# Weight sums kept in DRAM as float32 and split on the way back, with re-laid DRAM rows, new planner constants and a wider warm-up

## The chip, the cores and the metric

The kernel runs on one core of a Trainium2 chip. The time is device microseconds of one execution, from the chip. A profiled execution gives a span (first to last instruction) and the work of each engine: PE (TensorE, matrix products), PEld (its weight loads), DVE (VectorE), ACT (ScalarE), POOL (GpSimd) and SP (SyncE, which here issues nearly all DMAs).

## The reference, cut to what matters

Everything is float32. Attention with random features comes first, then two feed-forward layers:

```
x = phi(q) @ (phi(k)^T v) / (phi(q) @ sum(phi(k)) + 1e-6)   # 4 batches, 8 heads, 576 tokens, head 64, 128 features
phi(x) = exp(x w - |x|^2/2 - max) / sqrt(128)
h = x @ w_in ; g = softplus(h) ; y = g @ w_out              # 2304 tokens, 512 -> 2048 -> 512
h = y @ w_in2 ; g = h * sigmoid(h) ; out = g @ w_out2       # the same sizes
```

## The kernel before, in words

A float32 product is made from three fp32r products. Each operand is held as a high part (the value rounded to fp32r by an ACT copy) and a low part (value minus high part, by a DVE subtraction, `diff`, line 285); the products high·high, high·low and low·high are added up in PSUM.

The matrix work has four stages, one after the other on PE. Stage 1 is `first_layer` (lines 849 to 851): x @ w_in, directly. Between its blocks stand the matmuls of attention (lines 291, 579, 583, 714, 745, 761, 779). Stage 2 is `second_product(0)` (line 977), stage 3 `first_product` (line 1225), stage 4 `second_product(1)` (line 983). Stages 2 to 4 use a 2x2 block scheme with seven products in place of eight (order 1, 5, 6, 2, 7, 3, 4). For it each pair of weight blocks is turned into seven sums, cells of 128x256. There are 24 pairs: eight for each of the three weight matrices, `(0,1)`, `(1,0)` and `(1,1)`.

`sums_of(m, k)` makes the seven cells of a pair. Two raw loads of 512 KB (line 359) hold the weights in a 64-bit form, out of which `unpack` makes float32 (one ACT operation, three DVE operations: lines 364, 368, 373, 378). Four DVE operations add and subtract (line 479). In `stage`, ACT (lines 454, 456) makes the high part of a sum and DVE (lines 285, 461) the low part, three times for two cells together and once for one cell that is negated, and SP stores both parts into the DRAM tensor `ws` (line 466): 256 KB for a cell, 168 cells. For the first 12 pairs the parts are collected in two larger tiles (tag `wb`, constant `APART`), for the others they go out in four stores.

The products load their weights back from `ws`, both parts, in 42 loads of 1 MB (lines 1104 and 1123: 14 for each of the stages 2, 3 and 4). `second_product` takes the weights in two halves `q`; a half is seven tiles, used by three units of tokens (`sc`), and its tiles come free one by one in the last of the three.

In stages 2 and 4 a unit loads four blocks of `gate` (line 899, 768 KB each), DVE combines them (line 910, 1536 columns), ACT and DVE split 14 half-products (lines 925 and 285, 768 columns each) into tiles of tag `wa`, of which there are seven. DVE and ACT take the results out of PSUM (lines 1018, 1024, 1037). In stage 3 the results are gated (lines 1235, 1240, 1245, 1251) and stored in `gate[1]` (line 1258, 192 KB each).

The order of the work on every engine is planned on the host. Each operation is put into an `Order` with its cost in microseconds, the operations it waits for, the buffers it takes and a due time; `Order.run` then plays all engines forward in time and always takes the operation that can start first (nearly equal starts: the earlier due time). A DMA costs its bytes at 360 GB/s plus 2.3 us. Due times come from constants: `BEGIN`, `EVERY` and `SHARE` for attention and stage 1, `PREP` for the 24 pairs, `EARLIER` for how long ahead weights are loaded. What the planner puts out is the program order; on the chip each engine keeps to it and waits on semaphores.

At the start (lines 321 to 325) PE runs two products of 384 columns on zeros ("warm-up", four matmul records) while the first inputs are loaded; the first projection (line 579) waits for `om_sb`.

Of the kernel before, what the change touches and what calls it, by code (L numbers as in the profile page):

```python
# [8 lines left out]
F32 = mybir.dt.float32  # L9
# [35 lines left out]
ROW = {1: 0, 2: 1, 6: 2, 3: 3, 7: 4, 5: 5, 4: 6}  # L45
# [4 lines left out]
STAY = 6.79  # L50
# [6 lines left out]
FROM = {"PE": 4.6, "ACT": 3.4, "DVE": 2.0, "SP": 0.8}  # L57
SLACK = 0.15
EARLY = 6
# [6 lines left out]
BACKLOG, SOON = 0.6, 13.16  # L66
EARLIER = (26.31, 42.98)
APART = 12
AHEAD, WAIT = 3.04, 4.21
RATE = 360e3  # L70
ARRIVE = 2.3
ISSUE = 0.5
BEGIN = 38.66
SHARE = (1.76, 1.19, 1.06, 0.07, 0.19)
PREP = (118.5, 128.9, 155.1, 144.2, 172.5, 186.4, 193.1, 218.5, 239.1, 242.1, 258.9, 272.1, 289.7, 296.7, 311.4, 322.8, 520.9, 537.5, 578.5, 584.0, 604.5, 622.5, 614.1, 638.6)
# [10 lines left out]
def on_dve(n):  # L86
    return (0.067 + n / 960, 0.15)
# [3 lines left out]
class Order:  # L91
# [5 lines left out]
    def add(self, eng, cost, fn, deps=(), due=None, alloc=(), uses=(), table=None, nbytes=0, after=0.0, loose=False, behind=None, wait=0.0, tiled=False, turn=None):  # L97
# [34 lines left out]
    def run(self):  # L132
# [70 lines left out]
        while len(order) < len(items):  # L203
# [63 lines left out]
def attention_moe_moe_kernel(  # L267
# [45 lines left out]
    ws = {m: dram.tile([NFP, 7, P, 2 * 256], F32, name=f"ws{m[0]}{m[1]}") for m in ((0, 1), (1, 0), (1, 1))}  # L313
# [33 lines left out]
    def unpack(layer, fc, io, raw_tag, into, tf, first, after, due=None):  # L347
# [5 lines left out]
        def views():  # L353
            u = s["raw"].bitcast(U32).rearrange("p (n t) -> p n t", t=2)
            return u[:, :, 0], u[:, :, 1]
# [5 lines left out]
        def scale():  # L361
            first()
            hif = s["raw"].bitcast(F32).rearrange("p (n t) -> p n t", t=2)[:, :, 1]
# [17 lines left out]
        a = add("SP", (ISSUE, 0), load, alloc=[traw], nbytes=P * DM * 8, after=after, due=due)  # L381
# [3 lines left out]
        return add("DVE", V5, sign, [d], uses=[traw, tf]), b  # L385

    def weights(fc, after):
# [20 lines left out]
        r, _ = unpack(0, fc, 0, "b4" if e else "rw", lambda: s["f"], tf, begin, after)  # L408
# [5 lines left out]
    def sums_of(m, k, due, apart):  # L414
# [6 lines left out]
        def begin():  # L421
            s["f"] = get("f", [P, 2, DM], F32, f"pair_{name}")

        def row(i):
            return s["f"][:, :, i * 256 : (i + 1) * 256] if io else s["f"][:, i, :].rearrange("p (j w) -> p j w", j=2)

        done, opened = [], None
        for e in range(2):
            r, b = unpack(layer, 2 * k + e, io, "rw", lambda e=e: s["f"][:, e, :], tf, begin if e == 0 else lambda: None, due - 45, due - 16 + 2 * e)
# [4 lines left out]
        kept[m, k] = []  # L434

        group = {}

        def stage(i, of, n, deps, neg, due):
            g = 4 * (i >= 4) if apart else i
            rows = (4, 3)[g // 4] if apart else n  # L440
            tag = "wb" if apart else "rw"
            opens = g not in group
            if opens:
                group[g] = dict(t=new(tag), ends=[], left=rows)
            q = group[g]
            ts = q["t"]
            w = 256 * n

            def high():
                if opens:  # L450
                    q["st"] = get(tag, [P, rows, 2, 256], F32R, f"st_{name}_{g}")
                st = q["st"][:, i - g : i - g + n]
                if neg:
                    nc.scalar.activation(st[:, 0, 0], of()[:, 0], AF.Copy, scale=-1.0)
                else:
                    nc.scalar.copy(st[:, :, 0], of())  # L456

            def low():
                st = q["st"][:, i - g : i - g + n]
                if neg:  # L460
                    nc.vector.scalar_tensor_tensor(st[:, 0, 1], of()[:, 0], -1.0, st[:, 0, 0].bitcast(F32), op0=ALU.mult, op1=ALU.subtract)
                else:
                    diff(st[:, :, 1], of(), st[:, :, 0].bitcast(F32))

            def store():
                nc.sync.dma_start(ws[m][k, g : g + rows].rearrange("o p w -> p o w"), q["st"].bitcast(F32).rearrange("p o h w -> p o (h w)"))

            a = add("ACT", on_act(w), high, deps + ([] if opens else [q["first"]]), alloc=[ts] if opens else [], uses=[tf] + ([] if opens else [ts]))
            if opens:
                q["first"] = a  # L470
            b = add("DVE", on_dve(w), low, [a], uses=[ts, tf])
            q["ends"].append(b)
            q["left"] -= n
            if not q["left"]:
                kept[m, k].append(add("SP", (ISSUE, 0), store, q["ends"], uses=[ts], nbytes=P * 256 * rows * 8, due=due))
            return b

        def one(out, a, b, op, deps):
            return add("DVE", on_dve(256), lambda: nc.vector.tensor_tensor(out(), a(), b(), op=op), deps, uses=[tf])

        def cell(i, j):
            return lambda: row(i)[:, j]

        u = stage(0, lambda: row(0), 2, done, False, due - 5)
        v = stage(6, lambda: row(1)[:, 1:2], 1, done, True, due - 4)
        s1 = one(cell(1, 1), cell(1, 0), cell(1, 1), ALU.add, [v])
        s3 = one(cell(1, 0), cell(0, 0), cell(1, 0), ALU.subtract, [s1])
        stage(4, lambda: row(1), 2, [s3], False, due - 2)
        s2 = one(cell(0, 0), cell(1, 1), cell(0, 0), ALU.subtract, [s3, u])
        s4 = one(cell(0, 1), cell(0, 1), cell(0, 0), ALU.subtract, [s2])  # L490
        stage(2, lambda: row(0), 2, [s4], False, due)
# [7 lines left out]
    def inputs(s, name, xT, xN, vs, fold, held, after):  # L499
# [31 lines left out]
        for i, (v, shape) in enumerate(vs or ()):  # L531
# [12 lines left out]

            lv.append(add("SP", (ISSUE, 0), load_v, rv if tw is here else [] if opens else lv[:1], alloc=[tv[i]] if opens else [], uses=[] if opens else [tv[i]], nbytes=P * VW * 4, after=after))

# [275 lines left out]
    def first_layer(sb):  # L822
# [4 lines left out]
        for fc in range(NFC):  # L827
# [44 lines left out]
            stored[0].setdefault(fc, []).append((cols[sb], cols[sb] + w, add("SP", (ISSUE, 0), store, [a1], due=due + c1 + 4, uses=[tg], nbytes=P * w * 4)))  # L872
# [4 lines left out]
    def second_product(layer, t0):  # L877
# [6 lines left out]
        def unit(q, sc, t0, tws, wload, wt):  # L884
# [6 lines left out]
            def load_b(i, j):  # L891
# [60 lines left out]
            t4 = combine("t", "t", b21, [got[1, 0]] + e2, [tt, tb[1, 0]])  # L952
# [9 lines left out]
            def product(p, r, c, due, deps):  # L962
# [5 lines left out]
                def run(s=s, wt=wt):  # L968
# [4 lines left out]
                    for k in range(2):  # L973
                        if layer == 0:
                            cs = slice(c * P, (c + 1) * P)
                            for a, h in ((0, 0), (0, 1), (1, 0)):
                                nc.tensor.matmul(o[:, :HW_], w[:, 2 * r + k, a, cs], g[:, k, h], start=one, stop=(k == 1 and a == 1), skip_group_check=True)  # L977
                                one = False
                        else:
                            for a in range(2 if c == 0 else 1):  # L980
                                ts = slice((2 * c + a) * P, (2 * c + a + 1) * P)
                                for h, v in ((0, 0), (0, 1), (1, 0)):
                                    nc.tensor.matmul(o[:, a * 256 : a * 256 + 256], g[:, k, h, ts], w[:, 2 * r + k, v], start=one, stop=(k == 1 and h == 1), skip_group_check=True)  # L983
# [19 lines left out]
            def fetch(c, i, j):  # L1003
# [7 lines left out]
                return add("SP", (ISSUE, 0), load, [partly[sc, c, i, j]], alloc=[ht], nbytes=P * wide[c] * 4)  # L1011
# [17 lines left out]
            def finish(p, x, c, i, j, dep, due):  # L1029
# [9 lines left out]
                if not final:  # L1039
                    partly[sc, c, i, j] = add("SP", (ISSUE, 0), lambda s=s: nc.sync.dma_start(part_of(c, i, j), s["h", c, i, j][:, :w]), [e], uses=[ht], due=due + 3, nbytes=P * w * 4)  # L1040
                elif layer == 0:
                    yready[sc, i, j, c] = add("SP", (ISSUE, 0), lambda s=s: nc.sync.dma_start(y_dram[sc, i, j, c], s["h", c, i, j][:, :w]), [e], uses=[ht], due=due + 3, nbytes=P * w * 4)
                else:
                    for a in range(2 - c):
# [7 lines left out]
                        for p0, n, r0 in rows:  # L1052
# [4 lines left out]
                            add("SP", (ISSUE, 0), store, [e], uses=[ht], due=due + 3, nbytes=n * 1024)  # L1057
# [38 lines left out]
        for q in range(NQ):  # L1096
            tws, wload, wt = {}, {}, {}
            for n, p in enumerate(chain):
# [3 lines left out]
                def load_w(p=p, q=q, wt=wt, tag=tag):  # L1102
                    w = wt[p] = get(tag, [P, KQ, 2, 256], F32R, f"w2_{layer}_{q}_{p}")
# [296 lines left out]
```

## Time and profile before

| | before |
|---|---|
| median of 3 runs | 868.63 us (866.46 to 871.35) |
| profiled execution: time / span | 866.67 us / 864.9 us |
| PE busy | 851.5 us, 98% of the span |
| DVE / ACT busy | 681.6 us (79%) / 542.5 us (63%) |
| DMA queue of SP | 253.36 MB, 85% of 16 engines |
| mean granted clock | 1.000 |

"Busy" is the time in which an engine executed something; ends of matmuls are modelled, so neighbouring records overlap. Times in the rows below are microseconds unless marked ns.

### The profile page before, as it was taken

The numbers are of one execution on the slowest core, as the hardware profiler recorded it, in microseconds if no ns is written. First come the engines' busy times: TensorE is split into PE (matmuls) and PEld (weight loads), VectorE is DVE, ScalarE is ACT, GpSimd is POOL, SyncE is SP. The second block draws the span as 40 slices with busy tenths as digits, with TensorE's granted clock in tenths as the row PEclk, the third lists the DMA queues.
The fourth block names the chain that finished last, engine by engine and source line by source line (L and its number), as shares of the span: only waits on it lengthen the run. The fifth ranks groups of instructions, "written<-read, shape, count | busy, mean of one in ns | idle before, by whom it ended". The sixth has DMA issues, their size and how long they took to land.

```text
span 864.9 us, 17428 instructions
## 1 busy us (share of the span) xinstructions
PE 851.5 (98%) x6492; PEld 801.8 (93%) x6492; DVE 681.6 (79%) x1264; ACT 542.5 (63%) x1088; POOL 1.2 (0%) x8
## 2 busy tenths in 40 slices
PE   8899999999999999999999999999999999999998
PEld 7688888888888899999999998999999999999998
DVE  4999989969997377999799943786754899768973
ACT  6977778768765566876575444766855646543430
POOL 0000000000000000000000000000000000000000
PEclk9999999999999999999999999999999999999999
DMA  9576899899989999979995899987699997799532
GB/s 319 203 240 181 259 314 333 305 348 331 311 297 362 344 345 397 366 258 308 358 324 195 279 354 390 328 291 258 224 317 345 383 352 247 252 348 348 167 117 74
DMA packets 150293, 254.54 MB, mean 294 GB/s; under 512 B 10816, under 2 KB 82624, under 8 KB 150208
## 3 DMA queue, kind: packets, MB, share of 16 engines
q1 hardware_dynamic: 150048, 253.36, 85.0%
q8 instruction: 51, 0.84, 0.4%
q14 instruction: 34, 0.28, 0.1%
q10 hardware_dynamic: 160, 0.07, 0.0%
HBM read 152.72 MB, written 100.66 MB: 293 GB/s over the span
## 4 chain that ended last, share of the span: by engine, by line
PE 89%; DMA 5%; DVE 4%; ACT 1%; issue 1%; SPq 0%; ACTq 0%; DVEq 0%
PE X L977 12%; PE X L983 12%; PE X L1225 8%; PE h L849 8%; PE h L851 8%; PE h L850 8%; PE Z L983 6%; PE Z L977 6%; PE Z L1225 4%; PE Y L983 3%; PE Y L977 3%; PE Y L1225 2%; PE pp_q L579 2%; PE pp_k L579 2%; PE pkv_k L291 2%; PE pn_q L291 2%
## 5 line engine op out<-in xcount | busy, mean ns | idle before, releaser
L849 PE MATMUL h<-x,wt 128*128 128x512 f32 (+1 forms) x328 | 123.4, 376 | 0.0
L851 PE MATMUL h<-x,wt 128*128 128x512 f32 (+1 forms) x328 | 119.6, 365 | 0.0
L850 PE MATMUL h<-x,wt 128*128 128x512 f32 (+1 forms) x328 | 119.4, 364 | 0.0
L1225 PE MATMUL X<-x_x,w 128*128 128x384 f32 x576 | 106.6, 335 | 2.7 <-ACT s L1235 2.4
L925 ACT CAST g<-b 128x768 fp32r<-128x768 f32 x96 | 78.3, 838 | 48.4 <-PE X L983 19.2
L983 PE MATMUL X<-w,g 128*128 128x256 f32 x864 | 107.0, 283 | 0.2 <-issue 0.2
L983 PEld LDWEIGHTS X<-w,g 128*128 128x128 f32 x864 | 105.1, 192 | 0.5 <-issue 0.3
L1225 PEld LDWEIGHTS X<-x_x,w 128*128 128x128 f32 x576 | 100.2, 188 | 3.7 <-ACT s L1235 3.1
L977 PE MATMUL X<-g,w 128*128 128x384 f32 x576 | 102.9, 334 | 0.0
L977 PEld LDWEIGHTS X<-g,w 128*128 128x128 f32 x576 | 100.1, 188 | 0.0
L925 ACT CAST g<-t 128x768 fp32r<-128x768 f32 x72 | 58.8, 834 | 65.3 <-DVE t L910 38.1
L285 DVE TENSOR_TENSOR g<-b,g 128x768 fp32r<-128x768 f32 x96 | 90.0, 951 | 11.1 <-ACT g L925 11.1
L285 DVE TENSOR_TENSOR g<-t,g 128x768 fp32r<-128x768 f32 x72 | 67.5, 953 | 21.0 <-ACT g L925 20.7
L849 PEld LDWEIGHTS h<-x,wt 128*128 128x128 f32 x328 | 61.9, 189 | 10.4
L851 PEld LDWEIGHTS h<-x,wt 128*128 128x128 f32 x328 | 61.9, 189 | 10.2
L285 DVE TENSOR_TENSOR st<-pair,st 128x512 fp32r<-128x512 f32 x72 | 48.9, 686 | 27.9 <-ACT st L456 27.8
L850 PEld LDWEIGHTS h<-x,wt 128*128 128x128 f32 x328 | 62.0, 189 | 8.6
L855 ACT COPY g<-h 128x512 f32<-128x512 f32 (+1 forms) x80 | 44.1, 559 | 28.7 <-PE h L851 20.2
L456 ACT CAST st<-pair 128x512 fp32r<-128x512 f32 x72 | 44.8, 629 | 19.3 <-DMA ws<-st 7.7
L983 PE MATMUL Z<-w,g 128*128 128x256 f32 x432 | 54.0, 283 | 0.2 <-DVE g L285 0.2
L1225 PE MATMUL Z<-x_x,w 128*128 128x384 f32 x288 | 53.8, 334 | 0.0
L983 PEld LDWEIGHTS Z<-w,g 128*128 128x128 f32 x432 | 52.8, 192 | 0.4 <-DVE g L285 0.4
(113 smaller groups left out, 1457.0 us busy)
## 6 DMA issues: line engine op xcount, KB each, us to landing
w<-ws SPq DMA_DIRECT2D x42, 1024.0 KB, 7.7
b<-gate SPq DMA_DIRECT2D x48, 768.0 KB, 7.5
raw<-in_w SPq DMA_DIRECT2D x64, 512.0 KB, 6.0
ws<-st SPq DMA_DIRECT2D x36, 512.0 KB, 5.1
gate<-s SPq DMA_DIRECT2D x96, 192.0 KB, 4.6
gate<-g SPq DMA_DIRECT2D x64, 256.0 KB, 5.0
ws<-st SPq DMA_DIRECT2D x12, 1024.0 KB, 7.0
ws<-st SPq DMA_DIRECT2D x12, 768.0 KB, 5.5
```

The lines of the kernel that those rows point to most:

```text
L285: nc.vector.tensor_tensor(o, a, b, op=ALU.subtract)
L291: nc.tensor.matmul(o[r], a[:, r], b, **flags)
L456: nc.scalar.copy(st[:, :, 0], of())
L579: nc.tensor.matmul(pp[j][:, q], s["xt"][r, c : c + P], om_sb[r, :], start=True, stop=not fold)
L849: nc.tensor.matmul(ph, wt[:, 0, cs], xt[:, 0, ts], start=(opens and cc == 0), stop=False, skip_group_check=part is not None)
L850: nc.tensor.matmul(ph, wt[:, 0, cs], xt[:, 1, ts], start=False, stop=False, skip_group_check=part is not None)
L851: nc.tensor.matmul(ph, wt[:, 1, cs], xt[:, 0, ts], start=False, stop=(cc == NCC - 1), skip_group_check=part is not None)
L855: nc.scalar.copy(s["g"][:, :w], s["h"][:, :w])
L925: nc.scalar.copy(g[:, :, 0], s[src][:, 2 * r : 2 * r + 2])
L977: nc.tensor.matmul(o[:, :HW_], w[:, 2 * r + k, a, cs], g[:, k, h], start=one, stop=(k == 1 and a == 1), skip_group_check=True)
L983: nc.tensor.matmul(o[:, a * 256 : a * 256 + 256], g[:, k, h, ts], w[:, 2 * r + k, v], start=one, stop=(k == 1 and h == 1), skip_group_chec ...
L1225: nc.tensor.matmul(s[x][:, :HW_], w[:, a, cs], xop[p][:, cc, h], start=(opens and cc == 0 and a == 0 and h == 0), stop=(cc == 1 and a == 1 ...
```

## The change

Five things change, none of them the number or the shape of the matmuls of stages 1 to 4.

1. `sums_of` no longer splits. It makes the seven cells in float32 (cells 0 to 3 in the tile `f`, 4 to 6 in the second raw tile, whose content is used up by then) with the same four DVE operations, and stores them in two DMAs (512 KB and 384 KB). `APART` and `stage` go. The sign of one cell is turned, and with it one subtraction on the side of the data.
2. Behind each of the 42 loads, now 512 KB, stand a new ACT copy and a new DVE subtraction over 1024 columns (`halve`), before the products may use the tile.
3. `ws` and `gate[1]` are laid out so that a load reads 4 KB (`ws`) or 6 KB (`gate[1]`) in a row for each partition, in place of 2 KB and 1.5 KB. Stores into `ws` write rows of 1 KB for `(0,1)` and `(1,1)`, of 4 and 3 KB for `(1,0)`.
4. The planner costs a DMA by bytes and by rows, and adds 0.97 us behind each DMA that starts after 40.33 us. Its constants are new.
5. The warm-up has 512 columns in place of 384.

```diff
-ROW = {1: 0, 2: 1, 6: 2, 3: 3, 7: 4, 5: 5, 4: 6}
+ROW = {1: 0, 2: 1, 7: 2, 4: 3, 5: 4, 6: 5, 3: 6}
-FROM = {"PE": 4.6, "ACT": 3.4, "DVE": 2.0, "SP": 0.8}
+FROM = {"PE": 5.2, "ACT": 3.6, "DVE": 2.0, "SP": 0.8}
-FIRST = {"k": "by", "q": "yy", "kv": "b", "flip": "b", "num": "b", "back": "y"}
+FIRST = {"k": "by", "q": "yy", "kv": "b", "flip": "b", "num": "y", "back": "y"}
-LEAD, TRAIL, EVERY, WINDOW_OF, FETCH = 0.05, 2.2, 3.13, 25.82, 24.95
+LEAD, TRAIL, EVERY, WINDOW_OF, FETCH = 0.05, 2.36, 2.85, 35.33, 27.18
-EARLIER = (26.31, 42.98)
-APART = 12
+EARLIER = (35.65, 27.02)
+PER_BYTE, PER_ROW = 2.44e-6, 6.35e-4
+MARGIN, FIRM = 0.97, 40.33
-BEGIN = 38.66
-SHARE = (1.76, 1.19, 1.06, 0.07, 0.19)
-PREP = (118.5, 128.9, ... 638.6)
+BEGIN = 29.9
+SHARE = (1.76, 1.19, 1.06, 0.18, 0.41)
+PREP = (105.6, 119.7, ... 635.2)
...
+        nbytes *= RATE * (PER_BYTE + PER_ROW / row)
-                it["end"] = wire + ARRIVE
+                it["end"] = wire + ARRIVE + (MARGIN if s > FIRM else 0.0)
...
-    gate = [dram.tile([NQ, KQ, 2, P, B * S], F32, name=f"gate{i}") for i in range(2)]
+    gate = [dram.tile([NQ, KQ, 2, P, B * S], F32, name="gate0"), dram.tile([NQ, 2, SC, 2, P, KQ, HW_], F32, name="gate1")]
-    ws = {m: dram.tile([NFP, 7, P, 2 * 256], F32, ...
+    ws = {m: dram.tile([P, NFP * 7, 256] if m == (1, 0) else [NQ, 7, P, KQ, 256], F32, ...
-    wz = get("b2", [P, 3 * P], F32, "wz")
+    wz = get("b2", [P, 2 * T], F32, "wz")
-    pw = get("bank", [P, 3 * P], F32, "pw")
+    pw = get("bank", [P, 2 * T], F32, "pw")
...
+        def keep(o, n, of, deps, t, due):
+            return add("SP", (ISSUE, 0), lambda: store(o, n, of), deps, uses=[t], nbytes=P * n * 1024, row=n * 1024 if m == (1, 0) else 1024, due=due)
+        s1 = one(4, 2, 3, ALU.add, done)
+        s3 = one(2, 0, 2, ALU.subtract, [s1])
+        s2 = one(5, 4, 0, ALU.subtract, [s1])
+        s4 = one(6, 1, 5, ALU.subtract, [s2])
+        kept[m, k] = [keep(0, 4, ..., [s3], tf, due - 1), keep(4, 3, ..., [s4], traw, due)]
+
+    def halve(w, tw, dep, cells, due=None):
+        def high():
+            nc.scalar.copy(w()[:, 0], w()[:, 1].bitcast(F32))
+        def low():
+            t = w()
+            diff(t[:, 1], t[:, 1].bitcast(F32), t[:, 0].bitcast(F32))
+        a = add("ACT", on_act(cells * 256), high, [dep], uses=[tw])
+        return add("DVE", on_dve(cells * 256), low, [a], uses=[tw], due=due)
...
-                    w = wt[p] = get(tag, [P, KQ, 2, 256], F32R, ...)
-                    nc.sync.dma_start(w.bitcast(F32)..., ws[wm][q * KQ : (q + 1) * KQ, ROW[p]]...)
+                    w = wt[p] = get(tag, [P, 2, KQ, 256], F32R, ...)
+                    nc.sync.dma_start(w[:, 1].bitcast(F32), ws[wm][q, ROW[p]])
+                wload[p] = halve(lambda p=p, wt=wt: wt[p], tws[p], wl, KQ)
```

## Rows read from the trace of the kernel before

**Rows 1.** The page: busy time of PE, and the DMA queue of SP.

```profile
PE 851.5 (98%) x6492; PEld 801.8 (93%) x6492; DVE 681.6 (79%) x1264; ACT 542.5 (63%) x1088; POOL 1.2 (0%) x8
q1 hardware_dynamic: 150048, 253.36, 85.0%
```

**Rows 2.** Waits of PE: what it waited for, us in total, times, longest.

```profile
PE px_q L779 <- DVE xn_q L771: 3.8, 3, 1.8
PE X L1225 <- ACT s L1235: 2.4, 2, 1.9
PE pw L325 <- POOL ident masks.py:199: 1.8, 1, 1.8
```

**Rows 3.** Busy time by stretch: start:end, length, PE, PEld, DVE, ACT, POOL, clock, DMA share, GB/s.

```profile
20.00:46.00 26.00, 21.26 (x337) 18.04 (x336) 24.97 (x84) 24.41 (x72) 0.00 (x0) 1.00 0.63 222
46.00:326.00 280.00, 280.00 (x2405) 237.77 (x2404) 235.27 (x568) 200.08 (x475) 0.00 (x0) 1.00 0.89 306
413.30:500.70 87.40, 87.40 (x506) 87.40 (x505) 79.52 (x113) 47.40 (x61) 0.00 (x0) 1.00 0.87 290
500.70:545.00 44.30, 42.38 (x245) 42.06 (x244) 15.83 (x30) 21.54 (x45) 0.00 (x0) 1.00 1.03 372
```

**Rows 4.** PE in order of time at the start: start, us, line.

```profile
1.81 2.93 PE L325 MATMUL pw<-wz,ident 128*128 128x384 f32 x4 [1.81 <-POOL ident masks.py:199]
5.21 0.80 PE L579 MATMUL pp_k<-om_sb,x_k 64*128 64x128 f32 x4 [0.47 <-ACT om_sb L320]
...
7.17 0.64 PE L579 MATMUL pp_k<-om_sb,x_k 64*128 64x128 f32 x4
7.60 0.64 PE L583 MATMUL pp_k<-neg_half,x_k 64*128 64x128 f32 x4
...
10.92 0.39 PE L583 MATMUL pp_k<-neg_half,x_k 64*128 64x128 f32 x4
11.14 0.39 PE L579 MATMUL pp_k<-om_sb,x_k 64*128 64x128 f32 x4
```

**Rows 5.** ACT in order of time: the first two exponentials of attention.

```profile
9.85 2.17 ACT L623 ACTIVATE phi_k<-pp_k,mn_k 128x128 f32<-128x128 f32 x8 [1.42 <-DVE mn_k L596]
12.51 2.17 ACT L623 ACTIVATE phi_k<-pp_k,mn_k 128x128 f32<-128x128 f32 x8 [0.49 <-DVE mn_k L596]
```

**Rows 6.** The chain that ended last, around 503 to 540 us.

```profile
502.95 11.38 DMA raw<-in_w
...
519.91 8.74 DMA ws<-st
...
530.80 8.68 DMA gate<-s
```

**Rows 7.** Groups of DVE and ACT: busy us, mean ns, idle before.

```profile
L285 DVE TENSOR_TENSOR g<-b,g 128x768 fp32r<-128x768 f32 x96 | 90.0, 951 | 11.1 <-ACT g L925 11.1
L285 DVE TENSOR_TENSOR st<-pair,st 128x512 fp32r<-128x512 f32 x72 | 48.9, 686 | 27.9 <-ACT st L456 27.8
L910 DVE TENSOR_TENSOR t<-b,b 128x1536 f32<-128x1536 f32 x12 | 21.0, 1752 | 1.0 <-DMA b<-gate 1.0
L1037 DVE TENSOR_TENSOR h<-X,h 128x384 f32<-128x384 f32 (+2 forms) x36 | 19.6, 552 | 13.1 <-PE X L983 8.8 <-PE X L977 4.3
L461 DVE SCALAR_TENSOR_TENSOR st<-pair,st 128x256 fp32r<-128x256 f32 x24 | 10.1, 419 | 4.2 <-ACT st L454 4.0
L925 ACT CAST g<-b 128x768 fp32r<-128x768 f32 x96 | 78.3, 838 | 48.4 <-PE X L983 19.2 <-PE Z L983 9.0 <-PE Y L983 5.2
L456 ACT CAST st<-pair 128x512 fp32r<-128x512 f32 x72 | 44.8, 629 | 19.3 <-DMA ws<-st 7.7 <-DVE pair L479 5.8 <-DMA b<-gate 4.2
L454 ACT ACTIVATE st<-pair 128x256 fp32r<-128x256 f32 x24 | 10.2, 425 | 7.3 <-DVE pair L378 4.3 <-DMA ws<-st 2.7
```

**Rows 8.** DMA issues: count, KB each, median us from issue to landing.

```profile
w<-ws SPq DMA_DIRECT2D x42, 1024.0 KB, 7.7
raw<-in_w SPq DMA_DIRECT2D x64, 512.0 KB, 6.0
```

More of the change, by code (lines that the diff above doesn't have):

```diff
@@ L95, in __init__, with add @@
         self.items = []
-    def add(self, eng, cost, fn, deps=(), due=None, alloc=(), uses=(), table=None, nbytes=0, after=0.0, loose=False, behind=None, wait=0.0, tiled=False, turn=None):
+    def add(self, eng, cost, fn, deps=(), due=None, alloc=(), uses=(), table=None, nbytes=0, after=0.0, loose=False, behind=None, wait=0.0, tiled=False, turn=None, row=2048):
         occ, lag = cost if isinstance(cost, tuple) else (cost, PIPE)
         i = len(self.items)
+        nbytes *= RATE * (PER_BYTE + PER_ROW / row)
         it = dict(
@@ L345, in attention_moe_moe_kernel, with unpack @@
     wready = {}
-    def unpack(layer, fc, io, raw_tag, into, tf, first, after, due=None):
+    def unpack(layer, fc, io, raw_tag, into, tf, first, after, due=None, rows=1):
         s = {}
@@ L380, in unpack @@
         opens = not tf["users"]
-        a = add("SP", (ISSUE, 0), load, alloc=[traw], nbytes=P * DM * 8, after=after, due=due)
+        a = add("SP", (ISSUE, 0), load, alloc=[traw], nbytes=P * DM * 8, row=4096, after=after, due=due)
         b = add("ACT", (0.575, 0.37), scale, [a], alloc=[tf] if opens else [], uses=[traw] + ([] if opens else [tf]))
@@ L384, in unpack @@
         d = add("DVE", V5, low_bits, [b, c], uses=[traw, tf])
-        return add("DVE", V5, sign, [d], uses=[traw, tf]), b
+        return add("DVE", V5, sign, [d], uses=[traw, tf]), b, (s, traw)
     def weights(fc, after):
@@ L433, in sums_of @@
             done.append(r)
[L434 to L488, printed above, removed]
@@ L489, in sums_of, with cell, one @@
-        s2 = one(cell(0, 0), cell(1, 1), cell(0, 0), ALU.subtract, [s3, u])
-        s4 = one(cell(0, 1), cell(0, 1), cell(0, 0), ALU.subtract, [s2])
-        stage(2, lambda: row(0), 2, [s4], False, due)
+        def cell(o):
+            return s["f"][:, o] if o < 4 else sr["raw"].bitcast(F32)[:, (o - 4) * 256 : (o - 3) * 256]
+        def one(o, a, b, op, deps):
+            return add("DVE", on_dve(256), lambda: nc.vector.tensor_tensor(cell(o), cell(a), cell(b), op=op), deps, uses=[tf, traw])
@@ new lines, in sums_of @@
+        s4 = one(6, 1, 5, ALU.subtract, [s2])
+        kept[m, k] = [
+            keep(0, 4, lambda: s["f"], [s3], tf, due - 1),
+            keep(4, 3, lambda: sr["raw"].bitcast(F32)[:, :768].rearrange("p (o w) -> p o w", o=3), [s4], traw, due),
+        ]
+    def halve(w, tw, dep, cells, due=None):
[6 more added lines that the diff above has]
+        return add("DVE", on_dve(cells * 256), low, [a], uses=[tw], due=due)
@@ L543, in load_v @@
                 nc.sync.dma_start(s["v", i], v)
-            lv.append(add("SP", (ISSUE, 0), load_v, rv if tw is here else [] if opens else lv[:1], alloc=[tv[i]] if opens else [], uses=[] if opens else [tv[i]], nbytes=P * VW * 4, after=after))
+            lv.append(add("SP", (ISSUE, 0), load_v, rv if tw is here else [] if opens else lv[:1], alloc=[tv[i]] if opens else [], uses=[] if opens else [tv[i]], nbytes=P * VW * 4, row=1040 if shape[1] == 4 else 2080, after=after))
         def square():
@@ L871, in first_layer @@
             a1 = add("ACT", on_act(w, True), evacuate, [g1], due=due + c1 + 1.6, alloc=[tg], uses=[th])
-            stored[0].setdefault(fc, []).append((cols[sb], cols[sb] + w, add("SP", (ISSUE, 0), store, [a1], due=due + c1 + 4, uses=[tg], nbytes=P * w * 4)))
+            stored[0].setdefault(fc, []).append((cols[sb], cols[sb] + w, add("SP", (ISSUE, 0), store, [a1], due=due + c1 + 4, uses=[tg], nbytes=P * w * 4, row=w * 4)))
     last = [None]
@@ L976, in run @@
                             for a, h in ((0, 0), (0, 1), (1, 0)):
-                                nc.tensor.matmul(o[:, :HW_], w[:, 2 * r + k, a, cs], g[:, k, h], start=one, stop=(k == 1 and a == 1), skip_group_check=True)
+                                nc.tensor.matmul(o[:, :HW_], w[:, a, 2 * r + k, cs], g[:, k, h], start=one, stop=(k == 1 and a == 1), skip_group_check=True)
                                 one = False
@@ L982, in run @@
                                 for h, v in ((0, 0), (0, 1), (1, 0)):
-                                    nc.tensor.matmul(o[:, a * 256 : a * 256 + 256], g[:, k, h, ts], w[:, 2 * r + k, v], start=one, stop=(k == 1 and h == 1), skip_group_check=True)
+                                    nc.tensor.matmul(o[:, a * 256 : a * 256 + 256], g[:, k, h, ts], w[:, v, 2 * r + k], start=one, stop=(k == 1 and h == 1), skip_group_check=True)
                                     one = False
@@ L1055, in store @@
                                 nc.sync.dma_start(out[r0 : r0 + n, cs], s["h", c, i, j][p0 : p0 + n, a * 256 : a * 256 + 256])
-                            add("SP", (ISSUE, 0), store, [e], uses=[ht], due=due + 3, nbytes=n * 1024)
+                            add("SP", (ISSUE, 0), store, [e], uses=[ht], due=due + 3, nbytes=n * 1024, row=1024)
                 return e
@@ L1257, in store @@
                     def store():
-                        nc.sync.dma_start(gate[1][fc // (2 * KQ), fc // 2 % KQ, fc % 2][:, lo : lo + HW_], s[key])
-                    stored[1].setdefault(fc, []).append((lo, lo + HW_, add("SP", (ISSUE, 0), store, [a], uses=[th], due=due + 2.5, nbytes=P * HW_ * 4)))
+                        nc.sync.dma_start(gate[1][fc // (2 * KQ), fc % 2, sc, j, :, fc // 2 % KQ], s[key])
+                    stored[1].setdefault(fc, []).append((lo, lo + HW_, add("SP", (ISSUE, 0), store, [a], uses=[th], due=due + 2.5, nbytes=P * HW_ * 4, row=HW_ * 4)))
                 def step(p, end):
```

67 lines of the change are left out of this document (35 added, 32 removed).

## The prediction, as it was put on record

> **What bounds the kernel now.** I read the page first: PE is busy for 851.5 of 864.9 us, while SP's queue fills 85% of the DMA engines' time [rows 1]. So the first question is what PE loses, not what the DMAs carry: the change touches no matmul behind the start, and all it can win is PE's idle time, 864.9 - 851.5 = 13.4 us, and the time at the start in which PE works at half speed. The waits of PE say whose idle time it is: 3.8 us for attention's normalised values, 2.4 us in stage 3 for ACT, 1.8 us before the warm-up [rows 2]. The stretches say where: from 46 to 326 us PE is busy for all 280 us, from 413.3 to 500.7 us for all 87.4; the idle time stands in 20 to 46 us (26.0 - 21.3 = 4.7) and 500.7 to 545 us (44.3 - 42.4 = 1.9) [rows 3]. In the first of these DVE is busy for 25.0 of 26.0 us, in the second DVE for only 15.8 and the DMA engines all the time, at 372 GB/s [rows 3]. The granted clock reads 1.00 in these rows, so the slow start has to be read from the pitch: a group of four projection matmuls starts each 0.43 us (7.17 to 7.60) and later each 0.22 us (10.92 to 11.14) [rows 4]. [...]
>
> **The change, part by part.** I sum against the profiled execution, 866.67 us, which lies 1.96 us under the median of the runs shown, 868.63.
>
> *Splits.* Removed are 72 ACT and 72 DVE operations over 512 columns and 24 each over 256: on ACT 44.8 + 10.2 = 55.0 us, on DVE 48.9 + 10.1 = 59.0 [rows 7]. Added are 42 of each over 1024 columns, a size that no row shows. From below it is bounded by the 768-column rows, 838 ns on ACT and 951 on DVE, from above by the 1536-column DVE row, 1752 [rows 7]. Along the line between the DVE rows 1024 columns cost 951 + 256 * (1752 - 951) / 768 = 1218 ns; on ACT the step from 512 to 768 columns, 838 - 629 = 209, gives 1047. So ACT gains 55.0 - 42 * 1.05 = 11 us, DVE 59.0 - 42 * 1.22 = 8 us. Neither engine bounds the stages, and PE covers both: priced at 0. They move, however, and that is the risk: each tile is now split between landing and first use, some 2.3 us longer on the path of a weight.
>
> *DMA.* 168 cells of 256 KB went out and came back 42 times 1 MB [rows 8]: 44.0 MB each way, now half of each. SP's queue drops from 253.4 to 209.3 MB, by bytes from 85% to 70% [rows 1]. A halved load does not land in half the time: 512 KB of raw weights take 6.0 us, 1 MB of sums 7.7 [rows 8]. Two 1 KB-row stores per pair stand in for stores of 2 KB rows; nothing here shows rows of 1 KB. At worst they move their half of the bytes in the old time and only the loads gain (85% to 78%), at best everything scales. I take 72%, nearer to the best, since the loads' rows become longer.
>
> Where does this reach PE? Around 503 to 540 us the last-ended chain runs through three DMAs of 11.4, 8.7 and 8.7 us, a raw load, a store of sums, a store into the gate tensor [rows 6], and ends in the single 1.9 us wait of stage 3 [rows 2]. An unhurried raw load lands in 6.0 [rows 8], so this place has DMA time behind other DMAs, and the sums' stores and loads are what is halved. I give back 1.9 us: bounds 0 (another buffer is late) and 2.4 (the whole row).
>
> *Gate layout.* The 24 loads of stage 4 read longer rows. No row of stage 3 or 4 shows PE waiting for a gate load, so this costs and gives 0 on PE; bounds 0.5 us either way.
>
> *Warm-up.* Four records over 384 columns take 2.93 us from 1.81 [rows 4]; at 4/3 the columns they take 3.9 and end at 5.7. The first projection now starts at 5.21 after 0.47 us of idle [rows 4], so it starts 0.5 us later, without a gap. If the clock rises at the same time as now, 0.5 us is lost. If it is high from the first group at 5.7, the 12 groups between 5.2 and 10.6 each give back 0.21: 2.5 - 0.5 = 2.0 won. [...] But PE's time is not what counts here: attention's path goes on through DVE and ACT, whose first two exponentials start at 9.85 and 12.51 after 1.42 and 0.49 us of waiting [rows 5]. ACT can win those 1.9 us and no more. I take 1.1.
>
> [...]
>
> *Planner.* `BEGIN` and `EVERY` set attention's first due times up to 9 us earlier, `FETCH` and `WINDOW_OF` let weights and the next block load earlier. In 20 to 46 us DVE is the full engine [rows 3], and it carries work that is not urgent there (unpacking, the next block's projections) beside the normalisation that PE waits for. Better order gives back up to the 3.8 us of that wait [rows 2]; worse order adds as much, bounds -3.8 to 3.8. Earlier due times act on just this; I take 2.0 won. `MARGIN` issues nothing and delays nothing by itself; it only makes the plan keep more room behind a load. For stalls that any new order leaves somewhere between 46 and 860 us, where there are now nearly none [rows 3], I add 0.3; bounds 0 and 5.
>
> Sum: 866.7 - 1.9 - 1.1 - 2.0 + 0.3 = 862.0. The runs shown lie between 0.2 below and 4.7 above the profiled time; with the DMA engines less full I add 0.8 in place of the 1.96: 862.8 us.
>
> **Rivals.**
>
> *Nothing reaches PE (chance 0.28).* The DMAs and splits were hidden already, the prologue stays full on DVE, and PE keeps its pitch from 46 us on. For it: PE's 280 of 280 us [rows 3]. Against it: the three slow DMAs [rows 6] and the slow clock [rows 4] are both on the chain. Only the 1.1 of the clock or so would come: 865.5, with the spread of the runs 865 to 869.
>
> *All of it comes back (0.20).* Clock 1.9, prologue 3.8, stage 3 2.4: 866.7 - 8.1 = 858.6. For it: each part is aimed at by a piece of the change. Against: DVE's 25.0 of 26 us in the prologue [rows 3].
>
> *Splits at the turn of the halves stall PE (0.12).* In stages 2 and 4 the seven tiles of the second half can only be loaded as the last unit of the first half lets go of them, so all seven splits fall into about one unit, 29.1 us (87.4 / 3) [rows 3]. There DVE must do 14 * 0.951 for the halves, 4 * 1.752 for the combinations, 7 * 1.22 = 8.5 new, and some 10 of the 14 results at 0.552 = 5.5 [rows 7]: 34.3 us in 29.1, 5.2 too much. Now, without the splits, it is 25.8 and fits. The seven buffers of the halves give PE a lead of half a unit, 14.6 us, so this bites only from the point where DVE enters the turn with less than 5.2 us of lead. For it: DVE is at 79.5 of 87.4 us in 413.3 to 500.7 already [rows 3]. Against: neighbouring records overlap, so demand is less than the sum of the means, and 7.9 us are free. Price without any lead: two turns at 5.2; with the clock and prologue terms still won, 862.0 + 1.9 + 10.4 = 874.3.
>
> That the change does not do what it says is no rival for the bytes, only for the clock: it may stay low until about 10.6 us as now, which is inside the first rival.
>
> **How the numbers follow.** My forecast has the chance 0.40, as a band of 860.5 to 865.5. A measurement can tell 0.5% (4.3 us) from no change: faster means under 864.3, slower over 873.0. Of the forecast's 0.40, 0.34 lies under 864.3 and 0.06 above; the full gain adds 0.20 to faster; "nothing reaches PE" is 0.28 of no change, the stall at the turns 0.12 of slower. Together: faster 0.54, same 0.34, slower 0.12. The range goes from 857 to 869.5, which leaves out the stall at the turns and a rest below. The time is the forecast's, 862.8.
>
> **What would show it.** Right: the projections' pitch is 0.22 us per group well before 10.6 us; the first exponentials start before 9.85 and 12.51; the wait for the normalised values is shorter than 3.8 us; no 1.9 us wait for ACT in stage 3; DMA share of SP's queue near 72%; 42 CASTs of 1024 columns of about 1.05 us on ACT and 42 subtractions of about 1.22 on DVE; PE without idle time from the end of attention's first block to the tail. Wrong: PE waiting for a weight's split in stages 2 to 4 (the rival at the turns if it is near the middle of stage 2 or 4); the slow pitch lasting as long as now; a first stage-1 matmul that starts later than now; or a time under 858, which would need gains in the stretches where PE has none to give.

## The result, and the profile after

| | before | changed |
|---|---|---|
| median of 6 runs | 868.48 us (866.46 to 871.35) | 859.24 us (859.05 to 859.95) |
| ratio | 1 | 0.9893 [0.9873, 0.9914] |
| profiled execution: time / span | 866.67 / 864.9 us | 859.45 / 857.7 us |
| PE busy, PE idle | 851.5, 13.4 us | 848.1, 9.6 us |
| SP's DMA queue | 253.36 MB, 85.0% | 209.31 MB, 72.3% |

The change wins 9.2 us, 1.1%. The forecast was 862.8, a gain of 5.8: the direction held and the time lies in the range, but outside the forecast's own band of 860.5 to 865.5, near the rival "all of it comes back" (858.6).

The page of the changed kernel, as in [rows 1]; the queue carries the 44 MB less that were counted (line numbers here and below are those of each run's own kernel):

```profile
PE 848.1 (99%) x6492; PEld 798.5 (93%) x6492; DVE 675.7 (79%) x1210; ACT 540.0 (63%) x1034; POOL 1.3 (0%) x8
q1 hardware_dynamic: 119200, 209.31, 72.3%
```

What PE waited for in the changed kernel, as in [rows 2] (total, times, longest). Nothing of stages 2 to 4 is left in this list, and the wait for attention's normalised values (`px_q`) is 0.8 + 0.3 us in place of 3.8:

```profile
PE pw L327 <- POOL ident masks.py:199: 1.9, 1, 1.9
PE px_q L757 <- DVE den_q L746: 0.8, 2, 0.6
PE pp_k L557 <- ACT om_sb L322: 0.7, 1, 0.7
...
PE px_q L757 <- ACT phi_q L601: 0.3, 1, 0.3
```

Stretches of the changed kernel (columns as in [rows 3]). PE is full from 46 us to the tail; the DMA engines in 500.7 to 545 us run at 85% in place of 103%. DVE is the engine to watch: in 384.2 to 413.3 us, one unit's length at the turn of the halves in stage 2, it is busy for 29.01 of 29.10 us, where it was busy for 25.24 before (last row, from the kernel before):

```profile
20.00:46.00 26.00, 22.64 (x314) 18.96 (x311) 24.96 (x80) 24.69 (x72) 0.00 (x0) 1.00 0.79 270
46.00:326.00 280.00, 280.00 (x2403) 237.66 (x2402) 203.27 (x498) 178.52 (x424) 0.00 (x0) 1.00 0.75 248
384.20:413.30 29.10, 29.10 (x170) 29.10 (x169) 29.01 (x32) 25.45 (x34) 0.00 (x0) 1.00 0.83 291
413.30:500.70 87.40, 87.40 (x506) 87.40 (x505) 86.31 (x118) 56.39 (x71) 0.00 (x0) 1.00 0.77 261
500.70:545.00 44.30, 44.30 (x258) 44.30 (x257) 34.29 (x61) 29.54 (x55) 0.00 (x0) 1.00 0.85 292
...
384.20:413.30 29.10, 29.10 (x170) 29.10 (x169) 25.24 (x27) 20.52 (x28) 0.00 (x0) 1.00 0.95 324
```

PE at the start of the changed kernel, as in [rows 4]. The groups of four start each 0.22 us from 7.16 on (before: 0.43 until about 10.6), although the projections start later, since `om_sb` came later in this execution. The first exponential starts at 9.42 us in place of 9.85, and twenty run without a wait between them, where it was eight:

```profile
1.92 3.67 PE L327 MATMUL pw<-wz,ident 128*128 128x512 f32 x4 [1.92 <-POOL ident masks.py:199]
6.31 0.49 PE L557 MATMUL pp_k<-om_sb,x_k 64*128 64x128 f32 x4 [0.72 <-ACT om_sb L322]
...
7.16 0.39 PE L557 MATMUL pp_k<-om_sb,x_k 64*128 64x128 f32 x4
7.38 0.39 PE L561 MATMUL pp_k<-neg_half,x_k 64*128 64x128 f32 x4
```

The splits in the changed kernel (columns as in [rows 7]) cost what was worked out, 1050 and 1218 ns:

```profile
L462 ACT CAST w<-w 128x1024 fp32r<-128x1024 f32 x42 | 44.1, 1050 | 6.5 <-DMA w<-ws 6.0 <-PE Z L955 0.3
L287 DVE TENSOR_TENSOR w<-w 128x1024 fp32r<-128x1024 f32 x42 | 51.0, 1218 | 16.4 <-ACT w L462 16.2
```

DMA issues of the changed kernel (count, KB, median us to landing). The halved load lands in 5.1 us [rows 8: 7.7], raw loads in 5.5 [6.0]:

```profile
raw<-in_w SPq DMA_DIRECT2D x64, 512.0 KB, 5.5
w<-ws SPq DMA_DIRECT2D x42, 512.0 KB, 5.1
```

Where the 7.2 us of the span went, by the start of the first matmul of each stage and of the last matmul (the length of a stage is, here and below, from its first matmul to that of the next):

| first matmul of | before | changed | gained so far |
|---|---|---|---|
| stage 1 | 45.9 | 43.5 | 2.4 |
| stage 2 | 325.8 | 323.1 | 2.7 |
| stage 3 | 500.6 | 497.8 | 2.8 |
| stage 4 | 678.9 | 672.6 | 6.3 |
| last matmul starts | 861.3 | 853.9 | 7.4 |

So 2.7 us come from the start, 3.5 from stage 3 (178.3 to 174.8 us) and 1.1 from stage 4 (182.4 to 181.3); 0.2 are lost again behind the last matmul. In two more profiled executions of the changed kernel stage 1 starts at 42.7 and 42.9, so the gain of the start is 2.4 to 3.2 us up to there; stages 2 to 4 take the same time within 0.1.

### The profile page after: what moved, and what is told of

The parts are those of the page before. It is cut to its first block, busy times and chain, and to the rows that moved or that the text cites. A ratio compares the mean times of both kernels' runs of the same rounds, so it can differ in the third digit from the quotient of the medians.

```text
span 857.7 us, 17221 instructions
## 1 busy us (share of the span) xinstructions
PE 848.1 (99%) x6492; PEld 798.5 (93%) x6492; DVE 675.7 (79%) x1210; ACT 540.0 (63%) x1034; POOL 1.3 (0%) x8
## 3 DMA queue, kind: packets, MB, share of 16 engines
q1 hardware_dynamic: 119200, 209.31, 72.3%
## 4 chain that ended last, share of the span: by engine, by line
PE 96%; ACT 2%; DVE 1%; DMA 1%; issue 0%; ACTq 0%; DVEq 0%
PE X L961 12%; PE X L955 12%; PE X L1205 12%; PE h L827 8%; PE h L829 8%; PE h L828 8%; PE Z L961 6%; PE Z L1205 6%; PE Z L955 6%; PE Y L961 3%; PE Y L1205 3%; PE Y L955 3%; PE pp_q L557 2%; PE pp_k L557 2%; PE pn_q L293 2%; PE pkv_k L293 2%
## 5 line engine op out<-in xcount | busy, mean ns | idle before, releaser
L287 DVE TENSOR_TENSOR w<-w 128x1024 fp32r<-128x1024 f32 x42 | 51.0, 1218 | 16.4 <-ACT w L462 16.2
L1225 ACT ACTIVATE s<-s 128x384 f32<-128x384 f32 x72 | 37.2, 525 | 27.7 <-DVE s L1220 27.3
```

The costliest lines, as they stand in the source:

```text
L287: nc.vector.tensor_tensor(o, a, b, op=ALU.subtract)
L1225: a = add("ACT", on_act(HW_), lambda: nc.scalar.activation(s[key], s[key], AF.Silu), [dep], uses=[th], due=due, table="silu")
```

## The experiments

Ratios are to the kernel before, on the same chip in the same group of runs; its median there was 869.3 to 869.8 us. The changed kernel ran in two of the three groups.

### The warm-up

Taken out of the changed kernel, twice, and put alone into the kernel before:

```diff
-    wz = get("b2", [P, 2 * T], F32, "wz")
+    wz = get("b2", [P, 3 * P], F32, "wz")
-    pw = get("bank", [P, 2 * T], F32, "pw")
+    pw = get("bank", [P, 3 * P], F32, "pw")
```

> The changed kernel with the warm-up back at 384 columns, all else as changed. Theory A (the longer warm-up raises PE's clock in time): groups of four projections start each 0.43 us again until about 10 us, the first stage-1 matmul comes 1 to 2.5 us after 43.5 us, and the time is 860.5 to 862 us against 859.2 (ratio to the kernel before 0.991 to 0.993). Rival B (the new order of the prologue did it, the clock is hidden behind ACT and DVE): the pitch is slow again, but the first stage-1 matmul comes within 0.5 us of 43.5 and the time within 0.5 us of 859.2 (ratio 0.989 to 0.990).

> The changed kernel with the warm-up at 384 columns once more, now beside the changed kernel on one chip: 1 to 1.6 us more than it, as the first look and the 1.6 us later first stage-1 matmul say; no difference, if the earlier 1.1 us were the difference between two chips.

> The kernel before with nothing but the warm-up at 512 columns. Theory A (clock): projections at 0.22 us per group from about 7 us on, the time 866 to 867.5 us against 868.5 (ratio 0.997 to 0.999). Rival B (prologue bound by ACT and DVE in the old order): ratio 0.9995 to 1.001. A third possibility, that the spread of the kernel before (866.5 to 871.4) comes from the moment at which the clock rises: then the spread here shrinks to about 1 us; if it comes from the DMAs, it stays near 4 us.

> The changed kernel itself, as the yardstick of this group: 859 to 860 us, ratio 0.988 to 0.991.

Measured: 860.47 us (ratio 0.9901 [0.9885, 0.9918]) in the first group, 860.02 (0.9883 [0.9860, 0.9905]) in the third, where the changed kernel itself had 859.35 (0.9873 [0.9850, 0.9897]). Its own runs lie between 858.92 and 859.83, those with 384 columns between 858.88 and 861.56. The first group has theory A's signs (slow pitch, first stage-1 matmul 1.6 us later) and a time just under its band; the third shows less than the 1 to 1.6 us expected. Alone in the kernel before, 512 columns give 0.9986 [0.9968, 1.0004], inside A's band of ratios, with an interval that holds B's too. That run's projections are fast from 6.5 us on and stage 1 starts at 44.7 in place of 45.9, but stage 2 at 326.0 as before: among other things PE waits 0.8 us for attention between 100 and 200 us.

The two profiled executions of the changed kernel with 384 columns differ at the start, though the kernel is the same. The first, as [rows 4], is slow until 10.8 us:

```profile
5.48 0.80 PE L557 MATMUL pp_k<-om_sb,x_k 64*128 64x128 f32 x4 [0.73 <-ACT om_sb L322]
...
9.99 0.64 PE L557 MATMUL pp_k<-om_sb,x_k 64*128 64x128 f32 x4
10.42 0.64 PE L561 MATMUL pp_k<-neg_half,x_k 64*128 64x128 f32 x4
```

PE at the start of the second:

```profile
6.12 0.49 PE L557 MATMUL pp_k<-om_sb,x_k 64*128 64x128 f32 x4 [1.37 <-ACT om_sb L322]
...
6.96 0.39 PE L557 MATMUL pp_k<-om_sb,x_k 64*128 64x128 f32 x4
7.18 0.39 PE L561 MATMUL pp_k<-neg_half,x_k 64*128 64x128 f32 x4
```

Here the pitch of 0.22 us was there by 7 us after a warm-up of 384 columns and 1.37 us without work. The first matmul of stage 1 comes at 45.1 in the one and 43.3 in the other. Over all runs here, the pitch is 0.22 us by 7.3 us in each of the ten profiled executions with 512 columns, and in one of the four with 384. So the longer warm-up goes with an early rise of the pitch. It is worth some 0.7 us in the median, which the two overlapping intervals do not tell from nothing, and about 1.6 between these two executions (spans 859.3 and 857.7 us). With the same 384 columns the pitch changed at 10.8 us in the one and by 7 us in the other; what set the moment, no run shows. The third possibility of the expectation fell: with 512 columns the kernel before still spreads from 863.8 to 870.0 us.

### Old constants, new data path; and the reverse

All planner constants of the kernel before in the changed kernel, without margin and cost by rows; and the new constants (those that its planner has) in the kernel before.

```diff
-PER_BYTE, PER_ROW = 2.44e-6, 6.35e-4
-MARGIN, FIRM = 0.97, 40.33
-BEGIN = 29.9
+PER_BYTE, PER_ROW = 1 / RATE, 0.0
+MARGIN, FIRM = 0.0, 40.33
+BEGIN = 38.66
...
```

> The changed kernel (float32 sums, split after the load, new rows, warm-up of 512) with all planner constants of the kernel before and without the margin and the cost by rows. Theory A (the halved DMA bytes end the waits of stage 3): stage 3 takes 174.7 to 175.5 us of PE, no wait over 1 us there, 860 to 863 us (ratio 0.990 to 0.994). Rival B (the new constants and the margin did it): stage 3 takes 177 us or more, 864 to 868 us (ratio 0.995 to 1.0).

> The kernel before (parts stored in fp32r pairs, 253 MB, old layout, warm-up of 384) with the new planner constants except the margin and the cost by rows, which its planner does not have. Theory A (data path and constants each give about half, and the constants' half lies in the prologue): the wait of PE for the normalised values falls from 3.8 to under 1 us, the first stage-1 matmul comes 1 to 2 us before 45.9, stage 3 keeps its waits; ratio 0.995 to 0.999. Rival B (the constants are fitted to the new data path): something else gets worse by more than the prologue gains, ratio above 1.0.

> The changed kernel itself, beside the others of this group on one chip: ratio to the kernel before 0.988 to 0.991, spread of its runs about 1 us where the kernel before spreads over 5 us or more.

| ratio to before | old constants | new constants |
|---|---|---|
| old data path | 1 | 1.0073 [1.0047, 1.0098] (875.28 us) |
| new data path | 0.9945 [0.9924, 0.9965] (863.94 us) | 0.9890 [0.9850, 0.9930] (859.37 us) |

(The cells come from two groups; the lower left one includes the longer warm-up.) Data path alone: 5.5 us. Constants alone: 5.9 us worse. Together 10. In the first of the two crossings stage 3 takes 175.9 us, without a wait over 0.4 us there, which is nearer to A than to B; the wait for the normalised values is back at 3.6 us, and the time lies between the two bands, 0.9 us above A's and next to B's. So with the old constants the new data path takes 2.4 of the 3.6 us out of stage 3. In the second that wait is 0.8 + 0.3 us, as A said, but stage 1 starts only 0.6 us earlier than before, and stage 2 at 326.5, 0.7 later. B holds: stage 2 takes 180.4 us in place of 174.8 and stage 4 186.0 in place of 182.4, and PE waits for the split halves of the data (`g`). Waits of PE in that run, without those of the start:

```profile
PE Z L977 <- DVE g L285: 1.9, 1, 1.9
...
PE Z L983 <- DVE g L285: 1.5, 1, 1.5
PE X L1225 <- ACT s L1235: 1.4, 1, 1.4
```

The constants fit the new data path. Which part of it (fewer bytes, the later splits, the rows) they need, this crossing does not tell.

### The bytes, given back

Each store and each load of sums issued twice, the second store into a tensor that nobody reads, the first load into the part of the tile that the split overwrites. Once with the changed kernel's order, once with an order planned for the doubled bytes.

```diff
+            nc.sync.dma_start(to2, of())
...
+                    nc.sync.dma_start(w[:, 0].bitcast(F32), ws[wm][q, ROW[p]])
                     nc.sync.dma_start(w[:, 1].bitcast(F32), ws[wm][q, ROW[p]])
```

In the planned version the `nbytes` of these stores and loads are doubled as well.

> The changed kernel with every store of sums issued twice (the second into a tensor that nobody reads) and every load of sums issued twice (the first into the part of the tile that the split overwrites); the plan is unchanged, the bytes are those of the kernel before, 253 MB. Theory A (bytes are what counts in stage 3): SP's queue is at 84 to 88%, PE waits 2 to 5 us more in stages 2 to 4, 861 to 864 us (ratio 0.991 to 0.995). Rival B (the order counts, bytes were hidden): under 0.5 us more than 859.2 (ratio 0.989 to 0.990).

> As the run with all stores and loads of sums doubled, but the planner is told the doubled bytes, so the order is made for them. Theory A (the bytes matter through the waits of stage 3, a few us): 861 to 866 us. Rival D (the 46 us of the run with the old plan are a price of the bytes themselves, since the DMA engines are full where the products need them): still 890 us or more.

With the old order 905.62 us (1.0422 [1.0401, 1.0444]): some ten times what A expected, and B is out. Told of the bytes, the planner gets 870.23 us (1.0019 [0.9992, 1.0046]), so most of the 46 us was an order that the transfers could not follow, not the transfers; but 10.9 us over the changed kernel remain, more than A's band. So with the bytes given back the whole gain is gone, but not where I expected it. Stage 3 takes 174.8 us there, without a wait, with the DMA engines as full as before (1.02 from 500.7 to 545 us, 1.03 in the kernel before); stage 2 takes 182.9 and stage 4 183.4. In stage 2 DVE is busy for 174.4 of the 182.9 us, and PE waits mostly for DVE's splits of the data. Stretches of the planned version, columns as in [rows 3], and the two longest waits of PE in stage 2, as in [rows 2]:

```profile
326.00:413.30 87.30, 83.69 (x479) 82.55 (x478) 81.75 (x112) 63.26 (x86) 0.00 (x0) 1.00 0.95 354
413.30:500.70 87.40, 85.16 (x486) 83.70 (x485) 85.67 (x112) 55.58 (x68) 0.00 (x0) 1.00 0.97 344
500.70:545.00 44.30, 44.30 (x257) 44.14 (x256) 34.83 (x62) 30.61 (x56) 0.00 (x0) 1.00 1.02 375
...
PE X L957 <- DVE g L287: 3.0, 4, 1.7
PE Y L957 <- DVE g L287: 1.3, 1, 1.3
```

This doubling issues 90 more DMAs than the changed kernel, which a doubling of the bytes alone would not; the 10.9 us are those of both.

### The splits, doubled

Both operations of each split done twice (the second DVE operation leaves the values as they are), with the plan unchanged.

```diff
             nc.scalar.copy(w()[:, 0], w()[:, 1].bitcast(F32))
+            nc.scalar.copy(w()[:, 0], w()[:, 1].bitcast(F32))
...
             diff(t[:, 1], t[:, 1].bitcast(F32), t[:, 0].bitcast(F32))
+            nc.vector.tensor_tensor(t[:, 1], t[:, 1].bitcast(F32), t[:, 1].bitcast(F32), op=ALU.max)
```

> The changed kernel with both operations of every split done twice (42 more ACT copies of 1.05 us, 42 more DVE operations of 1.22 us; the plan is unchanged). Theory A (the lead of the halves' buffers covers the splits): PE waits at most 1 us more, 859 to 861 us. Rival C (DVE is at its limit at the turn from the first to the second half of the weights in stages 2 and 4, where it was busy for 86 of 87 us): waits of 3 to 10 us near 400 to 440 and near 750 us, 864 to 875 us.

898.37 us (1.0330 [1.0291, 1.0369]), far past A and past the band of C. Stage 2 takes 190.0 us, stage 3 191.2, stage 4 188.5, so the loss is not only at the turns. In stage 2 DVE is busy nearly all the time; this is the stretch of stage 2 in that run:

```profile
326.00:512.00 186.00, 177.07 (x987) 175.00 (x986) 180.10 (x233) 131.90 (x168) 0.00 (x0) 0.97 0.75 253
```

So a second set of splits, 51 us of DVE work, costs 39 us, while the first set shows no wait of PE. Of the 39, 12 are not idle time: PE is busy for 860.4 us in place of 848.1, at a granted clock of 0.97 in this stretch. And the plan was not told of the second set; for the bytes, telling it took 35 of 46 us away, and for the splits this was not tried. So the 39 us are no price of the DVE work alone. That the cover is nearly used up in stage 2 is seen without this run: in the changed kernel DVE is busy there for 171.6 of 174.7 us.

### The margin

```diff
-MARGIN, FIRM = 0.97, 40.33
+MARGIN, FIRM = 0.0, 40.33
```

> The changed kernel with the planner's margin behind loads set to 0, all else as changed. Theory A (the margin is not what gives the gain, the lead of the loads is long enough): 859 to 860.5 us, ratio 0.988 to 0.991. Rival B (without it the order is too tight and PE waits for a load): waits of over 0.5 us in stages 2 to 4, 861 to 866 us.

867.25 us (0.9975 [0.9953, 0.9998]) beside 859.35 for the changed kernel: B, by more than its band. Stage 2 takes 176.5 us in place of 174.7, stage 3 178.8 in place of 174.8: a loss as large as that of stage 3 in the kernel before is back, with half the bytes. PE in that run, in order of time, then ACT:

```profile
504.80 1.20 PE L1205 MATMUL X<-x_x,w 128*128 128x384 f32 x6
507.85 1.51 PE L1205 MATMUL X<-x_x,w 128*128 128x384 f32 x6 [1.84 <-ACT s L1215]
509.15 3.65 PE L1205 MATMUL Y<-x_x,w 128*128 128x384 f32 x12
512.64 2.24 PE L1205 MATMUL X<-x_x,w 128*128 128x384 f32 x12
...
506.37 1.04 ACT L462 CAST w<-w 128x1024 fp32r<-128x1024 f32 x1 [2.11 <-DMA w<-ws]
507.32 0.47 ACT L1215 COPY s<-X 128x384 f32<-128x384 f32 x1
```

The wait has the name of the one in [rows 2], PE for ACT's copy `s` out of PSUM, but another cause. There the chain ran through a slow raw load and a store into the gate tensor [rows 6]. Here ACT stood for 2.11 us before its new copy of a weight tile (line 462), and the copy that PE needed comes behind it in ACT's order. The load that ACT waited for was not slow: it landed in 5.9 us, where the median of these loads in the run is 5.8. It was issued late, at 500.5 us, 0.1 us before stage 3 began, behind a store of results; in the changed kernel the same load, the ninth of stage 3, is issued 2.6 us before, and ACT does not wait there. So here the margin acts through the order in which loads are issued.

Behind the wait twelve matmuls take 3.5 us from start to start in place of 2.1; the granted clock of 500.7 to 545 us is 0.96 in that run. Not all of this execution's loss is of this kind: 1.2 of its 7.2 us lie at the start (stage 1 at 44.1 us, 42.9 in the changed kernel beside it), where the granted clock is 0.96 from 0 to 46 us. The 12 runs spread from 864.3 to 870.6 us.

### The constants of the prologue

```diff
-BEGIN = 29.9
-FIRST = {"k": "by", "q": "yy", "kv": "b", "flip": "b", "num": "y", "back": "y"}
+BEGIN = 38.66
+FIRST = {"k": "by", "q": "yy", "kv": "b", "flip": "b", "num": "b", "back": "y"}
...
```

Also back to their old values: `STAY`, `FROM`, `SLACK`, `EARLY`, the line of `EVERY`, `AHEAD` and `WAIT`, `SHARE`.

> The changed kernel with the constants of attention and stage 1 of the kernel before (STAY, FROM, SLACK, EARLY, FIRST, BEGIN, EVERY and its line, WAIT, SHARE), the others, the margin and the data path as changed. Theory A (of the about 4.5 us that the constants give with the new data path, the prologue's order gives 1 to 2.5): PE waits 3 to 4 us for the normalised values again, first stage-1 matmul 1 to 2 us after 43.5, 861 to 862.5 us. Rival B (the constants of the later stages give it): under 0.5 us more than the changed kernel beside it.

863.78 us (0.9925 [0.9902, 0.9948]), 4.4 us over the changed kernel beside it, more than A's 1 to 2.5. The wait for the normalised values is back, and two waits in stage 1 join it; stages 2 to 4 take as long as in the changed kernel:

```profile
PE px_q L757 <- DVE xn_q L749: 3.6, 3, 1.6
...
PE pp_k L557 <- DVE x L287: 1.2, 1, 1.2
PE h L829 <- DVE wt L287: 0.7, 1, 0.7
```

Stage 1 starts at 44.1 us (changed kernel beside it: 42.9), stage 2 at 326.4 (322.5).

## Why the prediction was right, and where its sizes were off

**What bounds it.** Right for the profiled execution: PE's idle time and the slow start were all there was to win in it, and PE has no idle time left between 46 us and the tail.

**Splits: price 0.** Right for one set, with 1050 and 1218 ns as worked out. But "PE covers both" holds with little to spare. The rival at the turns had put all seven splits and some ten results into one unit. In the changed kernel 384.2 to 413.3 us hold five splits and six results, the other two splits come at 420 and 424 us, and DVE is full but PE does not wait. The risk named with the price, a longer path of a weight, did show where the margin was taken out: there ACT waits 2.11 us at a split, and PE 1.84 us behind it.

**DMA: 1.9 us.** The bytes (72% taken, 72.3% measured) were right, and the wait of stage 3 went, but the term is too small in two ways. First, the loss of stage 3 was 3.6 us (178.3 against the 174.7 of 1008 matmuls at 0.1733 us), not the 1.9 of its longest wait. These are PE's three waits there in the kernel before, the first with the rows ahead of it and behind (start, us):

```profile
535.93 2.24 PE L1225 MATMUL Y<-x_x,w 128*128 128x384 f32 x12
540.09 2.38 PE L1225 MATMUL X<-x_x,w 128*128 128x384 f32 x12 [1.92 <-ACT s L1235]
542.31 2.24 PE L1225 MATMUL Z<-x_x,w 128*128 128x384 f32 x12
...
658.52 1.33 PE L1225 MATMUL X<-x_x,w 128*128 128x384 f32 x6 [0.53 <-ACT s L1235]
...
677.75 1.34 PE L1225 MATMUL X<-x_x,w 128*128 128x384 f32 x6 [0.21 <-DVE s L1240]
```

The idle record of 1.92 us begins at the modelled end of the matmuls ahead (535.93 + 2.24 = 538.17 us). From start to start, twelve matmuls take 2.08 us; here 4.16 and then 2.22, so that the wait cost 2.22 us for a record of 1.92, some 0.3 more; the other two cost 0.83 and 0.51 for records of 0.53 and 0.21. Second, stage 4 held another 1.1 us that I had priced at 0. It takes 181.3 us in each of the eight profiled executions of the changed kernel with its bytes and splits as they are, whatever the constants, and 183.4 with the bytes given back; what the longer rows of `gate[1]` do there was not tried alone. Nor do bytes alone decide over stage 3: with half of them it takes 175.9 us on the old constants, 174.8 on the new ones and 178.8 on the new ones without the margin, and with all of them and a plan made for them 174.8. It takes an order that leaves the loads their time; in the runs here only the halved bytes had one that lost nothing in another stage.

**Warm-up: 1.1 us.** Right in kind (pitch 0.22 us by 7.3 us in all ten executions with 512 columns); 0.7 us in the median, as far as two overlapping intervals tell. That the pitch would change earlier was my estimate, and that it follows a clock was my reading: no run shows what sets the moment, and the granted clock reads 1.00 from 5.2 to 10.6 us in the kernel before, where the pitch is 0.43.

**Planner: 2.0 us.** Right in place, the wait for the normalised values, and under-sized: the old constants of the prologue cost 4.4 us, since stage 1's waits come with them. In the kernel before, the new constants shortened that wait as much, but lost more in stages 1, 2 and 4 (875.28 us). The step that failed is "`MARGIN` issues nothing and delays nothing by itself; it only makes the plan keep more room behind a load", priced at nothing: without that room the changed kernel loses 7.9 us. A plan without it issued a load of stage 3 so late that a landing time near the median was a wait of ACT and of PE.

**New stalls: 0.3 us.** None showed in the profiled executions of the changed kernel; measured 0.

**The spread: 0.8 added.** Too much: the median lies 0.2 us under the profiled execution. The changed kernel's runs agree within 2 us over all groups (858.9 to 860.7), those of the kernel before spread from 861.4 to 874.5. Of the runs here the spread is wide where PE still waits in stages 2 to 4 (6.3 us without the margin, 4.9 with doubled bytes) and narrow where it does not (0.9 to 2.7 us). So I infer that the median of the kernel before contains 2 to 3 us of such loss above its profiled execution, which went too. Two records support it. In the profiled execution of the kernel before with the longer warm-up (869.62 us) stage 3 took 181.5 us in place of 178.3, at a granted clock of 0.97 from 500.7 to 545. And of the 56 runs of the kernel before in the three groups, the 19 with a mean granted clock of 0.999 or 1.000 have a median of 868.4 us, the 23 with 0.996 or less 870.1. So part of the spread goes with the clock, and what set it in each run is open.

**How near it came.** The forecast lies 3.6 us too high: some 1.6 of it in stage 3, 1.1 in stage 4 and 1.0 in the spread; the rest cancels. That "all of it comes back" lies nearer is luck: of its 8.1 us it had 5.7 at the start and 2.4 in stage 3, where 2.7 and 3.5 came, and it had nothing for stage 4 and the spread.

The terms do not add: the margin, the prologue's constants and the halved bytes are each worth 4 to 11 us when taken out of the changed kernel, 23 together, while all of them give 9. Which of the single constants matter was not tried, nor were the new rows by themselves, nor the planner's cost by rows.

## What to carry to other kernels

When the busiest engine is at 98%, read its loss stage by stage from start-to-start times against the ideal pitch, not from idle records, and look for where an engine stands in its program order at an operation that needs a load: a margin behind loads in a static plan was worth more here (7.9 us) than any single wait in the list. A change of data path and a re-made plan belong together; either alone may show half the gain, or a loss. And a cost that seems hidden can be tested by doubling it, but tell the plan of it: with the bytes, three quarters of what the doubling cost was the plan that did not know.

## What was not expected of the hardware

With the same 384-column warm-up the pitch of 0.22 us came at about 10.8 us in one execution and by 7 us in another, the latter with 1.37 us without work just ahead. [rows 3] begin at 20 us, behind the slow stretch; but the column of the granted clock reads 1.00 in that stretch of the kernel before too, so only the pitch (0.43 against 0.22 us) told it (columns as in [rows 3]):

```profile
5.20:10.60 5.40, 5.39 (x50) 5.38 (x52) 1.29 (x2) 2.95 (x7) 0.00 (x0) 1.00 1.02 343
```

Without the margin, a single wait of 1.84 us in stage 3 was followed by twelve matmuls at 0.29 us in place of 0.17, so it cost 3.7 us in all. The wait of 1.92 us in the kernel before was not followed by such a stretch (twelve matmuls in 2.22 us) and cost 2.2.
